# Converting the second half's w_out under attention and keeping it in DRAM

## The chip, the cores and the metric

The kernel runs on one core of a Trainium2 chip. Its engines work from queues of their own: TensorE (PE; its weight loads are listed as PEld), VectorE (DVE), ScalarE (ACT), GpSimd (POOL), and SyncE (SP), which here only issues DMA transfers. Times are device microseconds (us), the median of several runs; a profile is one execution.

## The reference

```python
# attention: 8 batches, 8 heads, 512 local and 32 global tokens, 64 per head
s_ll = where(|i - j| <= 32, q_l k_l^T / 8, -1e9)      # a band of keys
out_l = softmax([q_l k_g^T / 8, s_ll]) [v_g, v_l]     # local tokens
out_g = softmax(q_g [k_g, k_l]^T / 8) [v_g, v_l]      # global tokens
# FFN over 4,352 tokens of 512, d_ff = 2048; weights and products at better than fp32r
h = x @ w_in                                          # 512 x 2048
g = h * erf(softplus(h))
out = g @ w_out                                       # 2048 x 512
```

## The kernel before

**Numbers.** The weights arrive as fp64 and are converted on the chip. A product of the accuracy wanted is made of three fp32r matmuls: each operand is split into a high part (`hi`, rounded) and a low part (`lo`, the rest), and hi x hi, hi x lo and lo x hi are added. `to_fp32` loads a block of 128 x 512 fp64 (`raw`, 524 KB), takes its magnitude on ScalarE and builds the fp32 value on VectorE from the bits (`top`); `split` makes the high part (a copy) and the low part (a subtraction on GpSimd or VectorE).

**Two halves.** The d_ff columns are worked in two halves of 1,024. The first half runs interleaved with attention. `attention` writes its result, transposed, to DRAM (`xsc`, and `xsg` for the global tokens); the tokens are then worked in nine chunks, one for each batch (512 tokens) and a last one of the 256 global tokens. For the first half `unit` multiplies by w_in, `gate` applies the function (two activation tables, each loaded anew), and `project` multiplies by w_out and stores the partial sum (`part`) from a staging tile `os`.

**The second half** takes the chunks in four pairs. Seven products of block sums replace the eight of a pair's first layer: `convert_in` makes the weight blocks and their sums and stores them in DRAM (`wq`), `pair_blocks` loads a pair's tokens (`rx`) and makes the sums and the splits, `products` does the matmuls in banks `pa` to `pd` and folds them on VectorE (`u`, `pair`). `project` multiplies by w_out, loads `part` into an `os` tile, adds, and stores the output. The last chunk (`last_blocks`, `last_unit`; names with `g`) uses four of the seven weight parts.

**Where the w_out of the second half is converted.** `load_unit` writes its parts into the buffers in which the first half's w_out lies, `oh` and `ol` of each of four units, so it can begin only when the first half has projected with that unit. That is at keys 71 to 74, the hand-over between the halves. The tokens of pair 1 wait in addition for three of these units (`AFTER`, `LAST`).

**Order.** Every operation is added with a key, a list of engines that could do it with a cost each, and what it reads and writes. `Program.schedule` plays this through once, before anything runs: at each moment a free engine takes the ready operation with the smallest key, if its buffers are free and its key isn't over 10.4 beyond the first one not done. The order found is written into the program, engine by engine, SP's transfers too. So a cost in these lists moves no work on the chip by itself, but it can change the order of everything. An instruction that waits holds what comes behind it on its engine. A buffer belongs to a tag with a fixed number of copies: `os` has four, `hs` and `sp` seven, `raw` five (raw weights and the tokens `rx` use the same), `wt` and `wr` one.

Of the kernel before, what the change touches and what calls it, by code (L numbers as in the profile page):

```python
# [20 lines left out]
P = 128  # L21
# [10 lines left out]
QLEAD, VLEAD, RLEAD, XLEAD = 0.755, 0.15, 0.011, 2.0  # L32
GOFF, POFF = 1.27, 4.29
WIN, WOUT = (-4.26, -3.26, -2.26, -1.26), (4.0, 5.0, 6.0, 7.0)
CV0, CVS, CVO = (46.5, 54.5), 1.8, (71.0, 72.0, 73.0, 74.0)
QLEAD2, XDEL = 4.0, 1.6
GATE1, GATE2, PROJ1, PROJ2 = (11.0, 17.0), (20.0, 25.0), 15.0, 23.0
LAST = (0, 2, 1)
BIAS, AHEAD = 0.65, 10.4

SLACK, PORT = {"PE": 0.8, "SP": 0.8}, 0.7
# [3 lines left out]
EARLY |= {f"va_0_{h}": ("hs" if h < 4 else "sp", 7) for h in range(8)}  # L45
EARLY |= {f"xT_0_{2 * p + 1}": ("gh", 5) for p in range(4)}
EARLY |= {f"vb_0_{h}": ("xh" if h % 2 == 0 else "xl", 3) for h in range(6)}
QUICK, WLEAD = 0, 0.011
LATER, GFIRST = 12, (-2.0, -1.7)
NORMAL = 1.125 * 2.0**-15  # L50
STRAIGHT = False
# [208 lines left out]
def kernel(  # L260
# [39 lines left out]
    act = lambda *a, **k: pinned(nc.scalar.activation(*a, **k))  # L300
    table = lambda name: pinned(nc.scalar.preload_act_table_set(name))  # L301
    dma = lambda *a, **k: pinned(nc.sync.dma_start(*a, **k))  # L302
    dma_act = lambda *a, **k: pinned(nc.scalar.dma_start(*a, **k))

    class Pin:
        def __init__(self, eng):
# [17 lines left out]
        b.ap = t  # L324
        return b

    def load(key, dst, src, kbytes, deps=(), also=(), quick=False):
        if quick:
            add({"ACT": 0.1}, key, lambda: dma_act(dst.ap, src), reads=deps, writes=[dst, *also], moved=kbytes)
            return  # L330
        add({"SP": 0.06}, key, lambda: dma(dst.ap, src), reads=deps, writes=[dst, *also], moved=kbytes)

    cs = attn.tile([P, 512 + P + 64 + 2], F32, name="cs")
    CS = fixed(cs)
# [21 lines left out]
    def abuf(shape, name, tag, bufs):  # L356
        if name in EARLY:
            tag, bufs = EARLY[name]
            b = Buf(mp, [P, 512 if tag in ("hs", "sp", "gh") else 1024], F32, name, tag, bufs)
            if bufs == 0:  # L360
                b.pool, b.bufs = wpool, 1
            b.view = shape
            return b
        return Buf(attn, shape, F32, name, tag, bufs)

    def psum_a(shape, name):
        return Buf(ps_a, shape, F32, name, "a", 6)

    def attention(b, h, key):
# [103 lines left out]
        if h % 2 == 1:  # L473
            XT = abuf([P, 4, P], f"xT_{nm}", "xT", 1)
            add({"DVE": 0.62},
                key + STEP * 4,
                lambda: dve.transpose(
                    XT.ap.rearrange("p j (t d) -> p j t d", d=WB), XN.ap.rearrange("p t (j d) -> p j t d", d=WB)
                ),
                [XN],  # L480
                [XT],
            )
            rows = xsc[b][P * p : P * p + P, :].rearrange("(j d) (a x) -> a d j x", d=WB, a=4)

            def store():
                for a in range(4):
                    (dma_act if b < QUICK else dma)(rows[a], XT.ap[WB * a : WB * a + WB])

            add({"ACT": 0.4} if b < QUICK else {"SP": 0.24}, key + STEP * 4, store, [XT, ATTN], [XSC[b, p]], moved=262.0)
        if h % 4 == 3:  # L490
            more = b, h // 4, [st["va", i] for i in range(4)], [st["qk", i] for i in range(2)]
            if b == 0 and LATER:
# [9 lines left out]
    def attention_global(b, j, VA, qk, key):  # L502
# [75 lines left out]
        def spread(e):  # L578
# [20 lines left out]
        )  # L599
        XT = abuf([P, 2, SG], f"gxT_{nm}", "gxT", 2)  # L600
        add({"DVE": 0.13, "ACT": 0.22}, key + STEP * 4, lambda e: copy(e, XT.ap.rearrange("p a q -> p (a q)"), X.ap), [X], [XT])
        add({"SP": 0.06},
            key + STEP * 4,
            lambda: dma(
                xsg[256 * j : 256 * j + 256, SG * b : SG * b + SG].rearrange("(a p) q -> p a q", p=P), XT.ap
# [4 lines left out]
        )  # L610

    st, W = {}, {}

    def mbuf(shape, dtype, name, tag, bufs):
        return Buf(mp, shape, dtype, name, tag, bufs)

    def to_fp32(key, src, name, TOP, ABS, deps, lead=RLEAD):

# [46 lines left out]
    def load_unit(kind, src, half, u, hi, lo, key, deps=(), lead=RLEAD):  # L665
# [5 lines left out]
            load_w(key + 0.01 * i, src[half, u, i], f"{kind}_{half}_{u}_{i}", HI, LO, i, deps, lead)  # L671
        W[kind, half, u] = (HI, LO)

    def load_x(ps, c, key):

        n = SL if c < B else B * SG
        X = []
        for i in range(2):
            RAW = mbuf([P, 2 * SL], F32, f"rx_{ps}_{c}_{i}", "raw", RAWS)
            HI = mbuf([P, 2 * SL], F32R, f"xh_{ps}_{c}_{i}", "xh", 3)  # L680
            LO = mbuf([P, 2 * SL], F32R, f"xl_{ps}_{c}_{i}", "xl", 3)
            for t in (RAW, HI, LO):
                t.view = [P, 2, n]
            src = (xsc[c] if c < B else xsg)[2 * P * i : 2 * P * i + 2 * P, :]
            deps = [XSC[c, p] for p in range(2 * i, 2 * i + 2)] if c < B else XSG
            load(key + 0.1 * i, RAW, src.rearrange("(k p) t -> p k t", p=P), 2.048 * n / 2, deps, quick=c < QUICK and ps == 0)
# [98 lines left out]
    def project(ps, c, G, at, order, after=None):  # L785
# [15 lines left out]
        for t in range(nt):  # L801
            for n, rows in enumerate(order):
                need = [x for g, _, v in rows for x in (*G[g], *W["out", ps, v // 2])]
                add(
                    {"PE": 0.685 * len(rows)},
                    at(n) + 0.01 * t,
                    lambda t=t, n=n: mm2(t, n),
                    list(dict.fromkeys(need)) + ([PART[after, t]] if after is not None and n == 0 else []),
                    [OP[t]],
                    heat=1536 * len(rows),  # L810
                )
            k = at(len(order) - 1) + 0.01 * t
            O = mbuf([P, DM], F32, f"os_{ps}_{c}_{t}", "os", 4)
            if ps == 0:
                add({"ACT": 0.58, "DVE": 0.69}, k, lambda e, t=t, O=O: copy(e, O.ap, OP[t].ap), [OP[t]], [O])
                add({"SP": 0.06},
                    k,
                    lambda t=t, O=O: dma(part[c][P * t : P * t + P, :], O.ap),
                    [O],
                    [PART[c, t]],  # L820
                    moved=262.0,
                )
            else:
                load(k - NU + 2, O, part[c][P * t : P * t + P, :], 262, [PART[c, t]])
                add({"DVE": 0.69},
                    k,
                    lambda t=t, O=O: dve.tensor_tensor(O.ap, OP[t].ap, O.ap, ALU.add),
                    [OP[t]],
                    [O, PART[c, t]],
                )  # L830
                add({"SP": 0.06}, k, lambda t=t, O=O: dma(out_rows(c, t), O.ap), [O], [fixed(None)], moved=262.0)

    class Late:

# [9 lines left out]
    for u in range(NU):  # L844
        load_unit("in", w_in, 0, u, (wpool, f"ih{u}"), (wpool, f"il{u}"), WIN[u], (), WLEAD)
        load_unit("out", w_out, 0, u, (wpool, f"oh{u}"), (wpool, f"ol{u}"), WOUT[u])

    def head_key(n):
        for (n0, k0), (n1, k1) in zip(HKEYS, HKEYS[1:]):
# [14 lines left out]
    def convert_in(u, key):  # L864
# [48 lines left out]
        for r, HL in enumerate(quads):  # L913
            for x, t in enumerate(HL):
                add(
                    {"SP": 0.06},
                    k + 0.6,
                    lambda x=x, t=t, q=2 * u + r: dma(wq[q][x], t.ap.bitcast(F32)),
                    [t],
                    [WQ[2 * u + r, x]],  # L920
                    moved=918.0,
                )
        return {2 * u + r: HL for r, HL in enumerate(quads)}


    def quad_weights(name, q, key):
        HL = [Buf(wb_pool, [P, 7, 2, P], F32R, f"wq{x}_{name}", f"q{x}", 2) for x in range(2)]
        for x, t in enumerate(HL):
            add(
                {"SP": 0.06},  # L930
                key,
                lambda x=x, t=t: dma(t.ap.bitcast(F32), wq[q][x]),
                [WQ[q, x]],
                [t],
                moved=918.0,
            )
        return HL

# [142 lines left out]
    def last_unit(q, X, key):  # L1081


        QH, QL = quad_weights(f"g{q}", q, key - QLEAD2)
        n = B * SG
        HP = Buf(ps_h, [P, 2, n], F32, f"h_g{q}", "h", 2)

# [33 lines left out]
    for u in range(2):  # L1121
        first = convert_in(1 - u, CV0[u])
    for n, u in enumerate((0, 2, 1, 3)):
        load_unit("out", w_out, 1, u, (wpool, f"oh{u}"), (wpool, f"ol{u}"), CVO[n], [ATTN])


    s0 = 17 * NU
    turns, ACTS = (), fixed(None)
    AFTER = {0: first[0], 1: [W["out", 1, u][1] for u in LAST]}
    for pr in range(B // 2):  # L1130
        s = s0 + 4 * NU * pr
        X = pair_blocks(pr, s - XDEL)
# [5 lines left out]
        order = [[(v, 0, v) for v in (2 * u, 2 * u + 1)] for u in (0, 2, 1, 3)]  # L1138
        for us, c, g, at in ((one, 2 * pr, GATE1, PROJ1), (two, 2 * pr + 1, GATE2, PROJ2)):
            G = {}  # L1140
            for h in range(2):
                turn = fixed(None)
                G |= gate(1, c, us[4 * h : 4 * h + 4], s + g[h], turns, [turn], [ACTS])
                turns = [turn]
            project(1, c, G, lambda n: s + at + 2 * n, order, c - 1 if c else None)
    s = s0 + 4 * NU * (B // 2)
# [83 lines left out]
```

## Time and profile before

| | |
|---|---|
| median of 3 runs (lowest, highest) | 957.44 us (957.0, 959.39) |
| the profiled execution: its time, its span | 959.59 us, 957.6 us |
| mean granted clock of TensorE | 0.982 |
| busy: TensorE, VectorE, ScalarE, GpSimd | 919.5, 650.2, 528.2, 401.7 us |
| moved by DMA | 168 MB, mean 175 GB/s |

The span is the time from the first to the last instruction; the run's time contains what lies around it. Matmuls overlap, so that the mean duration of one (about 390 ns for 512 columns) is longer than the distance between two. Names of tiles stand without their numbers: `top_out` is the fp32 value made of a w_out block, `wouth` and `woutl` its parts, `op` the bank of a projection, `o` that of attention's value product, `va` and `vb` its value tiles.

### The profile page before, as it was taken

To read this page: it belongs to the slowest core of one execution; us is meant where nothing else is said; L and a number is where in the kernel's file an instruction comes from. 1 tells how busy PE (TensorE), PEld (TensorE's weight loads), DVE (VectorE), ACT (ScalarE), POOL (GpSimd) and SP (SyncE) were. 2 spreads that over 40 slices of the span, in tenths; PEclk is the share of its full clock that TensorE was granted. 3 is DMA by queue.
4 is the path that set the end of the run, shared out by engine and by line. 5 is a ranking of instruction groups with operands and counts; after the bars stand their busy time and mean duration, and the time that the engine had idled before them with its cause. 6 is when DMAs were issued, how large, how long until landed. Compare 5 with 4: busy or idle time off the path is not lost.

```text
span 957.6 us, 22226 instructions
## 1 busy us (share of the span) xinstructions
PE 919.5 (96%) x8938; PEld 740.7 (77%) x8938; DVE 650.2 (68%) x1496; ACT 528.2 (55%) x868; POOL 401.7 (42%) x293
## 2 busy tenths in 40 slices
PE   8988899999989999999999999989999999999996
PEld 6666677777777777778888887767888888888885
DVE  4998889747856675855767799789656446544462
ACT  2547757455735545645765772657528445742850
POOL 1334645323313253312555683266537537521240
PEclk9999899999989999999999999989999999999999
DMA  9886577445864653724242453751742734334622
GB/s 345 290 292 206 185 228 239 135 118 180 253 196 122 214 183 94 237 53 146 88 186 78 173 201 120 284 189 43 287 165 78 252 135 183 121 144 165 231 89 88
DMA packets 86078, 168.00 MB, mean 175 GB/s; under 512 B 12888, under 2 KB 38488, under 8 KB 85976
## 3 DMA queue, kind: packets, MB, share of 16 engines
q1 hardware_dynamic: 85976, 166.60, 51.2%
q8 instruction: 70, 1.15, 0.5%
q14 instruction: 32, 0.26, 0.1%
HBM read 132.48 MB, written 34.08 MB: 174 GB/s over the span
## 4 chain that ended last, share of the span: by engine, by line
PE 71%; DVE 14%; DMA 9%; SPq 2%; issue 2%; ACT 1%; POOL 1%; DVEq 0%; ACTq 0%
PE op L298 33%; PE h L298 15%; PE pc L298 4%; PE pd L298 4%; PE pa L298 3%; PE o L298 3%; DVE top_out L311 2%; PE t L299 2%; PE s L298 2%; SPq L302 2%; PE pb L298 2%; DMA vb<-in_vB_dram 2%; DMA k<-in_kE_dram 2%; DVE xl_T L311 2%; DVE sp L311 1%
## 5 line engine op out<-in xcount | busy, mean ns | idle before, releaser
L298 PE MATMUL op<-wouth,gh 128*128 128x512 f32 x544 | 217.9, 401 | 0.0
L298 PE MATMUL op<-wouth,gl 128*128 128x512 f32 x544 | 212.8, 391 | 0.1
L298 PE MATMUL op<-woutl,gh 128*128 128x512 f32 x544 | 212.6, 391 | 0.0
L311 POOL TENSOR_TENSOR gl<-sp,gh 128x512 fp32r<-128x512 f32 x69 | 98.9, 1437 | 139.1 <-ACT gh L300 75.7
L300 ACT ACTIVATE gh<-sp 128x512 fp32r<-128x512 f32 x103 | 63.2, 628 | 106.9 <-PE op L298 75.9
L298 PEld LDWEIGHTS op<-wouth,gh 128*128 128x128 f32 x544 | 102.6, 189 | 23.2 <-issue 1.8
L298 PEld LDWEIGHTS op<-wouth,gl 128*128 128x128 f32 x544 | 102.4, 188 | 22.4 <-DVE gl L311 0.5
L311 POOL TENSOR_TENSOR sm<-sm,mx 128x512 f32<-128x512 f32 x41 | 45.4, 1113 | 174.6 <-DVE mx L311 125.0
L298 PEld LDWEIGHTS op<-woutl,gh 128*128 128x128 f32 x544 | 102.7, 189 | 19.5
L301 ACT ACT_TABLE_LOAD x90 | 115.5, 1283 | 2.3 <-PEq L1217 0.7
L298 PE MATMUL h<-xh,winh 128*128 128x512 f32 (+1 forms) x288 | 114.5, 398 | 0.0
L298 PE MATMUL h<-xl,winh 128*128 128x512 f32 (+1 forms) x288 | 111.0, 385 | 0.0
L298 PE MATMUL h<-xh,winl 128*128 128x512 f32 (+1 forms) x288 | 111.0, 385 | 0.0
L311 DVE TENSOR_TENSOR gl<-sp,gh 128x512 fp32r<-128x512 f32 x67 | 64.6, 969 | 37.3 <-ACT gh L300 33.7
L311 POOL TENSOR_TENSOR sp<-sp,hs 128x512 f32<-128x512 f32 x41 | 61.2, 1512 | 38.7 <-ACT sp L300 38.7
L300 ACT ACTIVATE sp<-sp 128x512 f32<-128x512 f32 x136 | 74.9, 620 | 0.4
L311 DVE CUSTOM_DVE_ANT_0 sm<-s,cs 128x128 f32<-128x128 f32 x256 | 57.1, 284 | 24.7 <-PE s L298 18.3
L300 ACT ACTIVATE hs<-h 128x512 f32<-128x512 f32 x49 | 29.3, 597 | 67.6 <-PE h L298 67.6
L298 PEld LDWEIGHTS h<-xh,winh 128*128 128x128 f32 x288 | 55.7, 193 | 11.3 <-issue 1.0
L298 PEld LDWEIGHTS h<-xh,winl 128*128 128x128 f32 x288 | 55.5, 193 | 11.4 <-issue 0.4
L298 PEld LDWEIGHTS h<-xl,winh 128*128 128x128 f32 x288 | 55.6, 193 | 9.6
L300 ACT ACTIVATE sm<-sm 128x512 f32<-128x512 f32 x64 | 39.3, 630 | 41.0 <-POOL sm L311 35.0
(181 smaller groups left out, 1844.9 us busy)
## 6 DMA issues: line engine op xcount, KB each, us to landing
wq<-wq SPq DMA_DIRECT2D x28, 896.0 KB, 6.3
vb<-in_vB_dram SPq DMA_DIRECT2D x64, 325.0 KB, 4.1
rx<-xsc SPq DMA_DIRECT2D x32, 512.0 KB, 7.6
va<-in_vA_dram SPq DMA_DIRECT2D x64, 195.0 KB, 3.6
k<-in_kE_dram SPq DMA_DIRECT2D x32, 384.0 KB, 5.8
q<-in_qT_dram SPq DMA_DIRECT2D x32, 272.0 KB, 4.7
part<-os SPq DMA_DIRECT2D x34, 256.0 KB, 3.0
os<-part SPq DMA_DIRECT2D x34, 256.0 KB, 3.7
```

The costliest lines, as they stand in the source:

```text
L298: pe = lambda n, *a, **k: pinned(nc.tensor.matmul(n, *a, **k))
L299: tr = lambda *a, **k: pinned(nc.tensor.transpose(*a, **k))
L300: act = lambda *a, **k: pinned(nc.scalar.activation(*a, **k))
L301: table = lambda name: pinned(nc.scalar.preload_act_table_set(name))
L302: dma = lambda *a, **k: pinned(nc.sync.dma_start(*a, **k))
L311: return lambda *a, **k: pinned(f(*a, **k))
```

## The change

The second half's w_out is converted by `keep_unit` at keys 20 to 37.5, in the middle of attention, into two `os` tiles a block, and stored in DRAM (`wo`, 16 stores of 262 KB). At keys 71 to 74 `fetch_unit` loads the finished parts (8 transfers of 524 KB) into the same `oh` and `ol` buffers as before. Pair 1's tokens no longer wait for it. Chunk 0 of the second half has three gates instead of two (2, 2 and 4 tiles, the first ones earlier). The last chunk's staging tiles carry the tag `hs`. Its weight loads take four of seven parts. And the planner counts 0.35 us of SP for each DMA, where it counted 0.06.

```diff
-LAST = (0, 2, 1)
+KEEP, KSTEP, FIRST = 20.0, 2.5, (6.0, 9.0)
+SPT = 0.35
...
-        add({"SP": 0.06}, key, lambda: dma(dst.ap, src), reads=deps, writes=[dst, *also], moved=kbytes)
+        add({"SP": SPT}, key, lambda: dma(dst.ap, src), reads=deps, writes=[dst, *also], moved=kbytes)
...
-            add({"ACT": 0.4} if b < QUICK else {"SP": 0.24}, key + STEP * 4, store, [XT, ATTN], [XSC[b, p]], moved=262.0)
+            add({"SP": 4 * SPT}, key + STEP * 4, store, [XT, ATTN], [XSC[b, p]], moved=262.0)
...
+    wo = [[dram.tile([P, 2, 512], F32, name=f"wo{u}_{x}") for x in range(2)] for u in range(NU)]
+    WO = {}
+
+    def keep_unit(u, key):
+
+        for i in range(2):
+            nm, k = f"k_out_{u}_{i}", key + KSTEP * i
+            TOP = View(mbuf([P, 512], F32, f"top_{nm}", ("wt", "wr")[i % 2], 1))
+            H, L = (View(mbuf([P, 512], F32R, f"{x}_{nm}", "os", 4)) for x in ("hi", "lo"))
+            to_fp32(k, w_out[1, u, i], nm, TOP, H, (), 1.0)
+            split(k, TOP, H, L)
+            for x, t in enumerate((H, L)):
+                WO[u, i, x] = fixed(None)
+                add(
+                    {"SP": SPT},
+                    k + 0.2,
+                    lambda x=x, t=t, i=i: dma(wo[u][x][:, i, :], t.ap().bitcast(F32)),
+                    [t.buf],
+                    [WO[u, i, x]],
+                    moved=262.0,
+                )
+
+    def fetch_unit(u, key):
+        parts = [Buf(wpool, [P, 2, 512], F32R, f"wout{x}_1_{u}", f"o{x}{u}") for x in "hl"]
+        for x, t in enumerate(parts):
+            add(
+                {"SP": SPT},
+                key,
+                lambda x=x, t=t: dma(t.ap.bitcast(F32), wo[u][x]),
+                [WO[u, i, x] for i in range(2)],
+                [t],
+                moved=524.0,
+            )
+        W["out", 1, u] = parts
...
-            O = mbuf([P, DM], F32, f"os_{ps}_{c}_{t}", "os", 4)
+            O = mbuf([P, DM], F32, f"os_{ps}_{c}_{t}", *(("os", 4) if ps == 0 or c < B else ("hs", 7)))
...
+    for u in range(NU):
+        keep_unit(u, KEEP + 2 * KSTEP * u)
...
-    def quad_weights(name, q, key):
+    def quad_weights(name, q, key, n=7):
...
-                lambda x=x, t=t: dma(t.ap.bitcast(F32), wq[q][x]),
+                lambda x=x, t=t: dma(t.ap[:, :n].bitcast(F32), wq[q][x][:, :n]),
...
-                moved=918.0,
+                moved=131.0 * n,
...
-        QH, QL = quad_weights(f"g{q}", q, key - QLEAD2)
+        QH, QL = quad_weights(f"g{q}", q, key - QLEAD2, S1 + 1)
...
-        load_unit("out", w_out, 1, u, (wpool, f"oh{u}"), (wpool, f"ol{u}"), CVO[n], [ATTN])
+        fetch_unit(u, CVO[n])
...
-    AFTER = {0: first[0], 1: [W["out", 1, u][1] for u in LAST]}
+    AFTER = {0: first[0]}
...
-            for h in range(2):
+            for a, z, at_z in ((0, 2, FIRST[0]), (2, 4, FIRST[1]), (4, 8, g[1])) if c == 0 else ((0, 4, g[0]), (4, 8, g[1])):
                 turn = fixed(None)
-                G |= gate(1, c, us[4 * h : 4 * h + 4], s + g[h], turns, [turn], [ACTS])
+                G |= gate(1, c, us[a:z], s + at_z, turns, [turn], [ACTS])
```

The other changed lines write `SPT` for 0.06 at the remaining DMAs and drop a second DMA queue that was switched off (`QUICK = 0`).

## Rows read from the trace of the kernel before

**Rows 1.** The page's head.
```profile
span 957.6 us, 22226 instructions
```

**Rows 2.** Stretch; busy (instructions) PE, PEld, DVE, ACT, POOL; clock, DMA share, GB/s.
```profile
264.00:432.00 168.00, 164.05 (x2300) 127.44 (x2300) 106.96 (x363) 86.17 (x148) 48.50 (x37) 0.98 0.50 156
...
570.00:672.00 102.00, 93.65 (x387) 74.96 (x386) 88.90 (x110) 56.67 (x91) 49.44 (x33) 0.95 0.42 161
672.00:888.00 216.00, 216.00 (x960) 179.07 (x959) 114.20 (x151) 105.62 (x163) 102.77 (x70) 1.00 0.46 167
...
276.00:288.00 12.00, 9.13 (x103) 7.41 (x92) 5.61 (x25) 5.10 (x11) 2.08 (x2) 0.72 0.62 201
```

**Rows 3.** TensorE's waits, 570 to 672 us, then after 880: total, times, longest.
```profile
PE pc L298 <- DVE pair L311: 4.3, 2, 3.9
PE pa L298 <- DVE u L311: 3.0, 1, 3.0
PE pd L298 <- DVE pair L311: 0.8, 1, 0.8
...
PE h_g L298 <- DMA wq_g<-wq: 1.8, 1, 1.8
```

**Rows 4.** VectorE's timeline: start, us, operation, out<-in; in brackets the idle time before.
```profile
613.38 1.56 DVE L311 TENSOR_SCALAR top_out<-raw_out 128x512 int32<-128x512 int32 x1
...
624.03 0.69 DVE L311 TENSOR_TENSOR pair<-u,pc 128x512 f32<-128x512 f32 x1
...
954.00 0.69 DVE L311 TENSOR_TENSOR os<-op,os 128x512 f32<-128x512 f32 x1 [5.01 <-DMA os<-part]
```

**Rows 5.** TensorE's timeline: a late value product, two hand-over gaps, the end.
```profile
279.45 0.41 PE L298 MATMUL o<-va,pt 128*32 128x65 f32 x3 [2.87 <-issue]
...
624.77 0.79 PE L298 MATMUL pc<-xh_B,wq 128*128 128x512 f32 x1 [3.87 <-DVE pair L311]
...
630.05 0.49 PE L298 MATMUL op<-wouth,gh 128*128 128x512 f32 x1
...
646.97 0.51 PE L298 MATMUL pa<-xh_B,wq 128*128 128x512 f32 x1 [3.00 <-DVE u L311]
...
650.95 0.40 PE L298 MATMUL pb<-xl_T,wq 128*128 128x512 f32 x1
...
949.23 0.39 PE L298 MATMUL op<-wouth,gl 128*128 128x512 f32 x1
```

**Rows 6.** Tile top_out, 560 to 672 us: busy by engine; durations min/median/max in ns.
```profile
560.00:672.00 112.00, 27.84 (x38) 3.74 (x6) 5.84 (x4) 0.95 0.43 161
...
L311 DVE SCALAR_TENSOR_TENSOR top_out<-raw_out,top_out x16: 691/693/1756, 582.2 to 628.6; 128x512 int32<-128x512 int32 x16
L311 DVE TENSOR_SCALAR top_out<-raw_out x8: 414/421/1565, 581.3 to 627.4; 128x512 int32<-128x512 int32 x8
```

**Rows 7.** SP's timeline of DMA issues: start, us, out<-in, count.
```profile
247.11 0.42 SPq L302 DMA_DIRECT2D k<-in_kE_dram  x1
...
273.76 1.98 SPq L302 DMA_DIRECT2D xsc<-xT  x4
276.15 0.83 SPq L302 DMA_DIRECT2D va<-in_vA_dram  x2
...
614.80 0.38 SPq L302 DMA_DIRECT2D raw_out<-in_w_out_dram  x1
615.27 4.41 SPq L302 DMA_DIRECT2D rx<-xsc  x4
```

**Rows 8.** The page's DMA issues: count, KB each, us to landing.
```profile
wq<-wq SPq DMA_DIRECT2D x28, 896.0 KB, 6.3
...
part<-os SPq DMA_DIRECT2D x34, 256.0 KB, 3.0
```

**Rows 9.** The chain that ended last: start, us, what.
```profile
891.41 8.67 DMA wq_g<-wq
...
944.93 6.02 DMA out_dram<-os
```

More of the change, by code (lines that the diff above doesn't have):

```diff
@@ L47 @@
 EARLY |= {f"vb_0_{h}": ("xh" if h % 2 == 0 else "xl", 3) for h in range(6)}
-QUICK, WLEAD = 0, 0.011
+WLEAD = 0.011
 LATER, GFIRST = 12, (-2.0, -1.7)
@@ L302 @@
     dma = lambda *a, **k: pinned(nc.sync.dma_start(*a, **k))
-    dma_act = lambda *a, **k: pinned(nc.scalar.dma_start(*a, **k))
     class Pin:
@@ L325, in fixed, with load @@
         return b
[L327 to L330, printed above, removed]
-        add({"SP": 0.06}, key, lambda: dma(dst.ap, src), reads=deps, writes=[dst, *also], moved=kbytes)
+    def load(key, dst, src, kbytes, deps=(), also=()):
+        add({"SP": SPT}, key, lambda: dma(dst.ap, src), reads=deps, writes=[dst, *also], moved=kbytes)
     cs = attn.tile([P, 512 + P + 64 + 2], F32, name="cs")
@@ L364, in abuf, with mbuf @@
         return Buf(attn, shape, F32, name, tag, bufs)
+    def mbuf(shape, dtype, name, tag, bufs):
+        return Buf(mp, shape, dtype, name, tag, bufs)
     def psum_a(shape, name):
@@ L486, in store @@
                 for a in range(4):
-                    (dma_act if b < QUICK else dma)(rows[a], XT.ap[WB * a : WB * a + WB])
-            add({"ACT": 0.4} if b < QUICK else {"SP": 0.24}, key + STEP * 4, store, [XT, ATTN], [XSC[b, p]], moved=262.0)
+                    dma(rows[a], XT.ap[WB * a : WB * a + WB])
+            add({"SP": 4 * SPT}, key + STEP * 4, store, [XT, ATTN], [XSC[b, p]], moved=262.0)
         if h % 4 == 3:
@@ L601, in attention_global @@
         add({"DVE": 0.13, "ACT": 0.22}, key + STEP * 4, lambda e: copy(e, XT.ap.rearrange("p a q -> p (a q)"), X.ap), [X], [XT])
-        add({"SP": 0.06},
+        add({"SP": SPT},
             key + STEP * 4,
@@ L612 @@
     st, W = {}, {}
-    def mbuf(shape, dtype, name, tag, bufs):
-        return Buf(mp, shape, dtype, name, tag, bufs)
     def to_fp32(key, src, name, TOP, ABS, deps, lead=RLEAD):
@@ L685, in load_x @@
             deps = [XSC[c, p] for p in range(2 * i, 2 * i + 2)] if c < B else XSG
-            load(key + 0.1 * i, RAW, src.rearrange("(k p) t -> p k t", p=P), 2.048 * n / 2, deps, quick=c < QUICK and ps == 0)
+            load(key + 0.1 * i, RAW, src.rearrange("(k p) t -> p k t", p=P), 2.048 * n / 2, deps)
             k = key + 0.1 * i + STEP * 2
@@ L812, in project @@
             k = at(len(order) - 1) + 0.01 * t
-            O = mbuf([P, DM], F32, f"os_{ps}_{c}_{t}", "os", 4)
+            O = mbuf([P, DM], F32, f"os_{ps}_{c}_{t}", *(("os", 4) if ps == 0 or c < B else ("hs", 7)))
             if ps == 0:
                 add({"ACT": 0.58, "DVE": 0.69}, k, lambda e, t=t, O=O: copy(e, O.ap, OP[t].ap), [OP[t]], [O])
-                add({"SP": 0.06},
+                add({"SP": SPT},
                     k,
@@ L830, in project @@
                 )
-                add({"SP": 0.06}, k, lambda t=t, O=O: dma(out_rows(c, t), O.ap), [O], [fixed(None)], moved=262.0)
+                add({"SP": SPT}, k, lambda t=t, O=O: dma(out_rows(c, t), O.ap), [O], [fixed(None)], moved=262.0)
     class Late:
@@ L915, in convert_in @@
                 add(
-                    {"SP": 0.06},
+                    {"SP": SPT},
                     k + 0.6,
@@ L929, in quad_weights @@
             add(
-                {"SP": 0.06},
+                {"SP": SPT},
                 key,
-                lambda x=x, t=t: dma(t.ap.bitcast(F32), wq[q][x]),
+                lambda x=x, t=t: dma(t.ap[:, :n].bitcast(F32), wq[q][x][:, :n]),
                 [WQ[q, x]],
                 [t],
-                moved=918.0,
+                moved=131.0 * n,
             )
```

## The prediction

> **What bounds the kernel now.** I read the page first, then a table of stages, then the waits of TensorE, then the engines' timelines around each wait.
>
> The span is 957.6 us [rows 1]. The profiled run took 959.59 us, about 2 us above the median of 957.44; the launch adds the same to both kernels, so I take every saving off the median. In the stage table [rows 2] the reader sees that TensorE never stops from 672 to 888 us: 960 matmuls in 216.00 us, 0.225 us each. That is what a stage costs when nothing is in its way, and nothing in this change takes a matmul away. So only gaps can be won. From 570 to 672 us, where the first half hands over to the second, TensorE is busy 93.65 of 102 us: 8.35 us idle. From 264 to 432 us, under attention, it is busy 164.05 of 168.
>
> The waits of the hand-over name one releaser, VectorE [rows 3]: 4.3 (3.87 and a second of 0.43), 3.0 and 0.8 us. VectorE's timeline shows why the longest lasted 3.87 us: from 613.38 us it works on `top_out`, the conversion of w_out, and the fold into `pair` for which TensorE needs its PSUM bank starts only at 624.03 [rows 4]. A gap costs twice. After it, the 12 matmuls from 624.77 to 630.05 us start 0.44 us apart instead of 0.225: the 1.2 GHz level, not the 2.4 GHz one [rows 5], so 5.28 - 2.70 = 2.6 us more. After the 3.00 us wait it is 10 matmuls from 646.97 to 650.95: 3.98 - 2.25 = 1.7 us. The hand-over thus loses 8.35 + 4.3 = 12.65 us. (387 matmuls at 0.225 us would fill 87.1 of the 102 us, which says 14.9; some records may be missing, so I use the smaller number.)
>
> **The change part by part.**
>
> *w_out leaves the hand-over.* The instructions on `top_out` take 27.84 us of VectorE from 560 to 672 us, with 3.74 of ScalarE and 5.84 of GpSimd [rows 6]; there VectorE is busy 88.90 of 102 us [rows 2]. All of it goes. The first wait (0.83, `pd`) and the 3.87 us wait sit behind it directly. The 3.00 us wait does so through a queue: pair 1's four `rx` loads were issued at 615.27, behind the last `raw_out` load at 614.80 [rows 7], because they had to wait for the conversion of three units and for staging buffers of the same tag. Their blocks were then built on VectorE in one run while TensorE waited for `u`. After the change the loads depend on neither. They can go out once pair 0's staging is free, and at the later hand-overs between pairs, where no conversion stands in the way, TensorE loses nothing from 672 to 888 us [rows 2].
>
> In its place come 8 fetches of 524 KB, the byte count of the 8 raw loads they replace. The page has 6.3 us for a landing of 896 KB and 3.0 for 256 KB [rows 8], so a fetch lands in 3 to 6 us. What follows is no conversion but the projection itself. The extra gate of chunk 0 adds two table loads, about 2.6 us of ScalarE, which is busy 56.67 of 102 us there [rows 2]: hidden, and at most 2.6 us if the last gate before chunk 0's second half of rows is on the path. What is late next? With VectorE down to some 61 of 102 us, pair 1's block building, which can't start before pair 0's last products release the tiles. I leave 2 us of gap for it (bounds 0 and 5.1, the last being the 3.00 us wait, its 1.7 of slow clock and that wait of 0.4). Gain 12.65 - 2.0 = 10.6.
>
> *Under attention.* Keys 20 to 37.5 are those of heads 41 to 59 of 64. The `k` of heads 42 and 43 is issued at 247.11 us [rows 7], so this lies between some 245 and 400 us, mostly in the stage of 264 to 432. Each of 8 blocks brings an Abs on ScalarE, one TENSOR_SCALAR and three SCALAR_TENSOR_TENSOR on VectorE, a copy and a subtraction. At the medians [rows 6] that is 0.42 + 3 x 0.69 = 2.5 us of VectorE a block, 20 us in all; with the subtractions and copies that fell to it before it was 28. VectorE has 168 - 106.96 = 61.0 us idle in that stage, ScalarE 81.8 and GpSimd 119.5 [rows 2]: hidden, unless it holds up something in order. The transfers are 8 loads of 524 KB and 16 stores of 262 KB, 8.4 MB beside the 156 GB/s x 168 us = 26.2 MB there; the DMA share would go from 0.50 to about 0.66. On SP's queue 24 issues at 0.41 us (two `va` in 0.83, [rows 7]) are 10 us of 168.
>
> The order matters more than the sums. Each store waits on SP for a ScalarE, VectorE or GpSimd result; behind it stand `va`, `vb`, `k` and `q`, for which TensorE waits. What that costs is in the trace: at 273.76 us four `xsc` stores stood ahead of two `va` loads, these were issued at 276.15, and the value matmuls started at 279.45, after 2.87 us of nothing, 3.3 us behind the issue [rows 5, 7]; the row names no releaser, so that it was this load is my reading. The 12 `h` matmuls behind it ran at the lower level (clock 0.72 from 276 to 288, [rows 2]), about 12 x 0.2 = 2.4 us: 5.3 us for one such stall. The stores also take two of the four `os` buffers, so an eviction can wait a landing, 3.0 us [rows 8]. Bounds 0 and 10.6 (two stalls); I take 2, nearer the low end, since TensorE waited for a load like that once in these 168 us.
>
> The trace shows how VectorE slows down when GpSimd works beside it: the same TENSOR_SCALAR takes 0.41 to 1.57 us, SCALAR_TENSOR_TENSOR 0.69 to 1.76 [rows 6]. If every conversion instruction met that, a block would cost 1.57 + 3 x 1.76 + 1.76 (a subtraction as slow) = 8.6 us, 69 us in all, more than the 61.0 idle. The page "SBUF — State Buffer" of the Trainium skill (section "Who interferes with whom") states this as a rule: VectorE with two SBUF inputs contends with a GpSimd instruction that reads SBUF, and whoever issues first blocks the other fully. It speaks against moving this work beside attention; by it the conversion would cost up to the 69 us, with the time of the rival below, and not the 28. The total of 27.84 us, measured with GpSimd at 49 of 102 us, against 48.5 of 168 under attention [rows 2], keeps me at 28.
>
> *The planner's 0.35 us for a DMA on SP.* No instruction changes, but the order does. The trace has about 0.41 us an issue; the planner counted 0.06, so ten queued transfers came over 3 us later than it planned. The stall just described is such a lateness. It may go (5.3 us) or not (0): I take half, 2.6.
>
> *The end.* The last matmul starts at 949.23 and ends near 949.6 [rows 5]. The last addition starts at 954.00, after 5.0 us of waiting for `os<-part` [rows 4]: with four `os` buffers for six tiles, the load had to wait for an output store issued at 944.93 that took 6.02 us [rows 9]. With the tags of `hs`, of which there are seven and by then few in use, the load can be early; the addition then starts at about 949.65. Gain 954.00 - 949.65 = 4.35.
>
> *The last weights.* 4 of 7 parts: each of 8 loads falls from 918 to 524 KB. Before, TensorE waited 1.8 us [rows 3] for a transfer that took 8.67 us on the chain [rows 9]; at 4/7 it is 3.7 us shorter. I take the whole 1.8 as gone (bounds 0, if the order and not the size is what is late, and 1.8).
>
> Sum: 10.6 + 4.35 + 1.8 + 2.6 - 2.0 = 17.35; 957.44 - 17.35 = **940 us** (against the profiled run's own 959.59 it is 942). At the bounds, with everything well: 12.65 + 4.35 + 1.8 + 5.3 = 24.1, 933. With everything ill but two stalls: 7.5 + 4.35 - 10.6 = 1.2, 956.
>
> **The rivals.**
> - *The hand-over closes only in part.* Against it: it is the conversion that stands in VectorE's timeline. For it: pair 1's blocks were built in one run of 14 us with TensorE waiting, and building them is not shortened. Gain 7.5 + 4.35 + 1.8 - 2 + 0: 946.
> - *The new stores hold SP under attention; slower.* Place 245 to 400 us, 5.3 us a stall. It decides from the fourth one, beyond the 19 us won elsewhere; with all of that won and five stalls it is 957.4 - 19 + 26.5 = 965. For it: one such stall exists already and 24 waiting DMAs are added. Against it: the planner now counts their time.
> - *VectorE fills up under attention.* If the conversion costs 69 us there, VectorE is full for 168 us, and TensorE loses as in the hand-over, 12.65 us in 102, so 20.8: 957.44 - 10.6 - 4.35 - 1.8 + 20.8, about 961. Against it: the smaller GpSimd share. The skill page's lock, named above, is what would do it.
> - *Fetches stand behind `wq` loads* that wait for products, so chunk 0 has no w_out until they move. Then the 12.65 us mostly stay, the rest is won: 951.
> - *The true SP cost mends more of attention* than this one stall: up to 6 us more, 934.
>
> **How the numbers follow.** 940 has 0.52, part-closed 0.20, stores on SP 0.07, VectorE full 0.04, late fetches 0.05, more mended 0.09, nothing to measure 0.03. About 0.3%, 2.9 us, is what a measurement can tell from no change. Faster: 0.52 + 0.20 + 0.05 + 0.09 = 0.86; same 0.03; slower 0.11. The range that leaves some 2 in 10 out goes from 933, the good bound, to 952, past the late fetches.
>
> **What would show it.** In the new profile: no `top_out` work of half 1 between 570 and 672 us; pair 1's `rx` issued some 20 us before pair 0's last products; no VectorE wait over 1 us at the hand-over and the clock at 1.00 throughout; `os<-part` no longer in the last 8 us; no wait for `wq_g`. It would be wrong if 245 to 400 us shows new waits of `o` or `s` for loads, each with a stretch of low clock, or if TensorE waits for the fetched `wout` tiles.

## The result, and the profile after

The changed kernel takes 945.65 us (median of 4 runs, 944.67 to 946.68); the kernel before took 958.41 us beside it on the same chip (4 runs, 957.0 to 960.14). The ratio is 0.9866, 95% interval 0.9844 to 0.9888: 12.8 us less, where I had forecast 17.4. The profiled execution took 945.86 us, at a mean granted clock of 0.991 (0.982 before).

The head of the page of the changed kernel answers to [rows 1]. Its matmul helper is now line 299, its VectorE helper still 311, its DMA helper 303.

```profile
span 944.1 us, 22303 instructions
```

The stage table of the changed kernel, columns as in [rows 2]: attention, the stall near 279 us, the hand-over, the stage between pairs, and a long stretch over both.

```profile
264.00:432.00 168.00, 166.02 (x2294) 128.31 (x2287) 120.87 (x380) 98.52 (x175) 54.88 (x42) 1.00 0.60 187
276.00:288.00 12.00, 11.81 (x194) 9.45 (x192) 10.19 (x33) 6.84 (x16) 4.33 (x3) 1.00 0.63 192
560.00:664.00 104.00, 102.01 (x448) 83.33 (x447) 70.78 (x75) 58.10 (x90) 54.07 (x34) 1.00 0.49 182
664.00:872.00 208.00, 208.00 (x920) 172.22 (x919) 114.22 (x154) 110.85 (x169) 103.36 (x72) 1.00 0.46 165
600.00:936.00 336.00, 336.00 (x1529) 280.08 (x1528) 184.00 (x240) 181.37 (x272) 152.45 (x103) 1.00 0.45 161
```

The hand-over is closed: TensorE idles 2.0 of 104 us where it idled 8.35 of 102, the clock stays at 1.00, and from 600 to 936 us there is no gap at all. VectorE is busy 70.78 us in place of 88.90, where some 61 had been forecast. The waits of TensorE from 560 to 700 us answer to [rows 3]:

```profile
PE pa L299 <- DVE c L311: 1.1, 1, 1.1
PE pd L299 <- DVE xl_T L311: 0.7, 1, 0.7
PE pc L299 <- DVE pair L311: 0.2, 1, 0.2
```

SP's timeline answers to [rows 7]: pair 1's `rx` go out at 592 and 597 us, not at 615, among the fetches of the kept w_out; the last line is the end, six output stores and nothing before them that waits.

```profile
592.46 0.37 SPq L303 DMA_DIRECT2D rx<-xsc  x1
595.87 0.32 SPq L303 DMA_DIRECT2D wouth<-wo  x1
...
596.77 1.41 SPq L303 DMA_DIRECT2D rx<-xsc  x3
...
606.75 0.32 SPq L303 DMA_DIRECT2D wouth<-wo  x1
...
927.84 12.57 SPq L303 DMA_DIRECT2D out_dram<-os  x6
```

TensorE's last matmul and VectorE's additions answer to the last lines of [rows 5] and [rows 4]. The additions follow TensorE (releaser `PE op`), no longer a load of `os<-part`; no wait for `wq_g` is left either.

```profile
938.93 0.39 PE L299 MATMUL op<-wouth,gl 128*128 128x512 f32 x1
```

```profile
938.00 0.69 DVE L311 TENSOR_TENSOR os<-op,os 128x512 f32<-128x512 f32 x1 [0.67 <-PE op L299]
939.36 0.69 DVE L311 TENSOR_TENSOR os<-op,os 128x512 f32<-128x512 f32 x1 [0.67 <-PE op L299]
```

The conversion now stands under attention, from 201 to 352 us. Its tile, with durations in ns as in [rows 6]; over the whole span the instructions on it take 28.20 us of VectorE.

```profile
0.00:960.00 960.00, 28.20 (x35) 3.16 (x5) 11.18 (x8) 0.99 0.54 180
...
L311 DVE SCALAR_TENSOR_TENSOR top_k_out<-raw_k_out,top_k_out x16: 691/693/1666, 201.4 to 342.8; 128x512 int32<-128x512 int32 x16
L311 DVE TENSOR_SCALAR top_k_out<-raw_k_out x8: 403/424/1343, 200.9 to 339.7; 128x512 int32<-128x512 int32 x8
L311 DVE SCALAR_TENSOR_TENSOR top_k_out<-hi_k_out,top_k_out x8: 674/694/1772, 202.9 to 350.7; 128x512 f32<-128x512 f32 x8
```

**Where the 13.5 us between the two spans went.** I cut both spans at two marks that TensorE's timeline gives. The last `h` matmul of the first half starts at 559.1 us before and 562.6 after: 3.5 us lost. From there to the start of the last matmul it is 390.13 us before and 376.37 after: 13.8 won. From the start of the last matmul to the end of the span it is 8.37 and 5.17: 3.2 won.

### The profile page after: what moved, and what is told of

It reads as the page before. It is cut to its first block, busy times and chain, and to the rows that moved or that the text cites. A ratio compares the mean times of both kernels' runs of the same rounds, so it can differ in the third digit from the quotient of the medians.

```text
span 944.1 us, 22303 instructions
## 1 busy us (share of the span) xinstructions
PE 914.6 (97%) x8937; PEld 736.0 (78%) x8937; DVE 643.0 (68%) x1484; ACT 536.0 (57%) x895; POOL 401.8 (43%) x295
## 3 DMA queue, kind: packets, MB, share of 16 engines
q8 instruction: 70, 1.15, 0.5%
## 4 chain that ended last, share of the span: by engine, by line
PE 79%; DVE 9%; issue 2%; DMA 1%; SPq 0%; ACT 0%; DVEq 0%
PE op L299 37%; PE h L299 16%; PE pc L299 4%; PE pd L299 4%; PE pa L299 4%; DVE top_out L311 3%; PE o L299 2%; PE s L299 2%; PE pb L299 2%; PE t L300 2%; PE h_g L299 1%; PE go L299 1%; PE ga L299 1%; DVE sm L311 1%; PE gt L300 1%
## 5 line engine op out<-in xcount | busy, mean ns | idle before, releaser
L311 POOL TENSOR_TENSOR gl<-sp,gh 128x512 fp32r<-128x512 f32 x66 | 92.7, 1409 | 111.7 <-ACT gh L301 70.0
L311 POOL TENSOR_TENSOR sm<-sm,mx 128x512 f32<-128x512 f32 x43 | 49.0, 1149 | 131.9 <-DVE mx L311 77.3
L311 DVE TENSOR_TENSOR gl<-sp,gh 128x512 fp32r<-128x512 f32 x70 | 70.7, 1019 | 38.6 <-ACT gh L301 37.3
L311 POOL TENSOR_TENSOR sp<-sp,hs 128x512 f32<-128x512 f32 x46 | 68.3, 1505 | 55.0 <-ACT sp L301 55.0
L301 ACT ACTIVATE hs<-h 128x512 f32<-128x512 f32 x44 | 26.2, 595 | 62.0 <-PE h L299 62.0
```

What stands on the lines that cost most here:

```text
L311: return lambda *a, **k: pinned(f(*a, **k))
```

## The experiments

Each ratio is to the kernel before, timed beside it on the same chip. Four parts of the change can be made alone, so I began with these.

**The SP cost alone.** The kernel before with one number changed wherever a DMA is planned:

```diff
-        add({"SP": 0.06}, key, lambda: dma(dst.ap, src), reads=deps, writes=[dst, *also], moved=kbytes)
+        add({"SP": 0.35}, key, lambda: dma(dst.ap, src), reads=deps, writes=[dst, *also], moved=kbytes)
```

> The kernel before with one edit: the planner counts 0.35 us of SP for each DMA and not 0.06. Theory 1 (the new order under attention is what costs the 3.5 us by which the changed kernel's first half ends later): 961 to 964 us, with TensorE losing more before 190 us than in the kernel before. Theory 2 (the moved conversion costs them; the true SP cost mends the late value load at 279 us): 953 to 957 us, and no stall near 279 us.

Measured: 968.87 us, ratio 1.0087 (1.0062 to 1.0111): 8.6 us slower; neither theory had that. The stall near 279 us was gone (TensorE busy 12.00 of the 12 us from 276), but the hand-over grew (96.73 of the 115 us from 565 to 680, before 106.65). SP's timeline of this kernel shows pair 1's four `rx` now ahead of the last `raw_out`, and TensorE's waits from 560 to 700 us show what it cost:

```profile
619.29 2.46 SPq L303 DMA_DIRECT2D rx<-xsc  x4
621.87 0.45 SPq L303 DMA_DIRECT2D raw_out<-in_w_out_dram  x1
```

```profile
PE pc L299 <- DVE c L312: 14.2, 2, 12.2
PE pc L299 <- DVE pair L312: 2.2, 3, 1.2
```

The last block of the conversion then ran at 637 to 649 us, amid pair 1's block building. A truer cost in the plan is not a gain by itself.

**Everything but the SP cost.** The changed kernel with `SPT = 0.06`.

> The changed kernel with the planner's SP cost back at 0.06 us. Theory 1: 941 to 943 us, the first half's last matmul at 558 to 560 us. Theory 2: 946 to 949 us, that matmul at 562 us or later.

Measured: 954.17 us, ratio 0.9935 (0.9914 to 0.9956), slower than both theories had it. With the conversion moved, the same cost that lost 8.6 us alone is worth some 6.6, by the difference to the changed kernel's ratio (0.0069 of 960 us; with the two intervals some 3 us either way).

**The conversion alone.** The kernel before with `keep_unit`, `fetch_unit` and the shorter `AFTER`; SP cost, gates and the end as before.

> The kernel before with the conversion moved under attention and the fetches, and nothing else of the change (SP cost 0.06, two gates for chunk 0, four staging buffers, seven weight parts). Both theories have the hand-over of 12.65 us closed to within 2. Theory 1: 946 to 948 us. Theory 2: 949 to 951 us. If the third gate of chunk 0 is what fills TensorE at the hand-over, TensorE still waits there for over 3 us: 950 or more, with the waits between 600 and 660 us.

Measured: 959.61 us, ratio 0.9986 (0.9969 to 1.0003): no change that can be measured, where the theories had 946 to 951. The hand-over closed here too (TensorE busy 112.35 of 115 us from 565 to 680, 106.65 before), but the last first-half `h` came at 569.2, 10 us later than before. All of the gain was given back under attention, and this kernel's VectorE timeline shows the place:

```profile
273.26 0.68 DVE L311 TENSOR_TENSOR gl<-sp,gh 128x512 fp32r<-128x512 f32 x1
303.06 0.29 DVE L311 CUSTOM_DVE_ANT_0 sm<-s,cs 128x128 f32<-128x128 f32 x1 [29.12 <-PE t L300]
```

VectorE had nothing for 29 us, because TensorE was given 34 us of `h` and `op` matmuls in one piece, from 268.2 us on. The longest such piece between 190 and 436 us is 8.3 us in the kernel before and 6.9 in the changed one (worked out from the starts in TensorE's timeline). SP's front DMA waited for a product behind that piece; SP's waits in this kernel, 190 to 360 us:

```profile
SPq L303 <- PE o L299: 42.6, 13, 29.1
```

TensorE itself was full meanwhile. The loss came afterwards, in attention. Two stretches, of this kernel and then of the changed one:

```profile
270.00:300.00 30.00, 30.00 (x134) 24.86 (x133) 3.94 (x4) 12.16 (x19) 7.62 (x6) 1.00 0.08 30
300.00:348.00 48.00, 38.64 (x753) 30.45 (x753) 37.93 (x132) 31.21 (x58) 21.13 (x17) 0.89 0.78 257
```

```profile
270.00:300.00 30.00, 28.88 (x420) 22.83 (x419) 24.59 (x71) 18.19 (x35) 14.16 (x10) 1.00 0.74 244
300.00:348.00 48.00, 47.75 (x688) 37.35 (x687) 36.84 (x113) 32.17 (x56) 15.55 (x12) 1.00 0.72 222
```

From 300 to 348 us 9.4 us are idle at a clock of 0.89, against 0.25 at 1.00.

**The two ends alone.** The kernel before with the last chunk's staging in the tags of `hs` and 4 of 7 parts of the last weights.

> The kernel before with the last chunk's staging under the tag of hs and four of seven weight parts for it, and nothing else. By the prediction 4.35 + 1.8 = 6.15 us less: 952.3 us. By what the new profile shows of the tail (3.2 us less from the last matmul to the end) and the whole 1.8: 953.4. If the order and not the size made the last weights late, the wait stays: 955.

Measured: 953.84 us, ratio 0.993 (0.991 to 0.9949): 6.4 us, against 4.35 + 1.8 = 6.15 forecast.

**Without the conversion's work.** The changed kernel, with the first half's w_out stored in place of a converted second half; it leaves out the 8 loads and all the work of the conversion, and has 8 stores of 524 KB:

```diff
-            to_fp32(k, w_out[1, u, i], nm, TOP, H, (), 1.0)
-            split(k, TOP, H, L)
...
+        for x, t in enumerate(W["out", 0, u]):
...
+                lambda x=x, t=t: dma(wo[u][x], t.ap.bitcast(F32)),
```

> The changed kernel without the conversion of the second half's w_out: neither its 8 loads nor any instruction on top_out and its parts; the first half's converted w_out is stored instead, in 8 stores of 524 KB at the same planned times (so the second half multiplies with the wrong weights: this asks only for time). Open question: of the 4.2 us that the sum missed (12.8 us won, 17.35 forecast), are they paid for the conversion under attention? Theory 1 (yes, the moved conversion costs some 4 us there, twice what I put down): the kernel comes out near 941 to 942, ratio to before 0.982. Theory 2 (attention differs only by how the plan falls out, and by some us from one execution to the next; the conversion is hidden): 945 to 947, ratio 0.986 to 0.988, with the last first-half h matmul still near 562 us.

Measured: 943.43 us, ratio 0.984 (0.9816 to 0.9864), 2.2 us below the changed kernel (2.5 by the ratios); the intervals overlap. The conversion costs 0 to some 5 us under attention, the middle of it where I had put it (2.0). It is hardly what the forecast missed, though the upper end isn't excluded; and this kernel, too, has an order of its own, which can be a part of the difference.

**Two gates for chunk 0.** The changed kernel with `for a, z, at_z in ((0, 4, g[0]), (4, 8, g[1]))` for every chunk.

> The changed kernel with two gates for chunk 0 of the second half, of four units each, as before, in place of three (two, two and four units). Theory 1 (the third gate hides: its two table loads on ScalarE cost nothing and chunk 0's projection was not waiting for the first gate): ratio 0.986 to 0.988, no change that can be told from the changed kernel, TensorE's hand-over from 565 to 680 us still with less than 3 us of waits. Theory 2 (with w_out already there, chunk 0's projection now starts as early as its gate allows, and the early gate of two units is what lets it): 3 to 6 us slower, ratio 0.990 to 0.993, and a TensorE wait of that size for g of chunk 0 between 590 and 625 us.

Measured: 947.95 us, ratio 0.9868 (0.9844 to 0.9892), as the changed kernel. The third gate neither costs nor brings anything that can be measured here, which means less than some 3 us.

**The rx loads freed, the conversion left where it was.** The kernel before with one dependency less:

```diff
-    AFTER = {0: first[0], 1: [W["out", 1, u][1] for u in LAST]}
+    AFTER = {0: first[0]}
```

> The kernel before, with one dependency taken off: pair 1's four rx loads no longer wait for the conversion of three units of w_out; the conversion itself stays at the hand-over. My prediction laid the 3.00 us wait for u (with its 1.7 us of slow clock and the small wait of 0.4) on these loads being late. Theory 1 (that is so): the rx loads go out some 15 to 20 us before 615 us, the wait of pa for u is gone, the 3.87 us wait stays, and the kernel gains up to 5 us, ratio 0.995 to 0.997. Theory 2 (VectorE is what is full there, so that the blocks, built earlier, only push the conversion later): ratio 0.999 to 1.003, and the waits grow somewhere else in the hand-over.

Measured: 965.94 us, ratio 1.0078 (1.005 to 1.0106): 7.5 us slower; neither theory had that. One of the four loads went out 8 us earlier, the other three did not. In SP's timeline the last raw block now falls behind them (before it went out at 614.80): as I read it, they take its staging tiles. TensorE's waits from 560 to 700 us (the three largest) move to what is built late:

```profile
607.37 0.39 SPq L302 DMA_DIRECT2D rx<-xsc  x1
...
615.51 2.03 SPq L302 DMA_DIRECT2D rx<-xsc  x3
620.04 0.35 SPq L302 DMA_DIRECT2D raw_out<-in_w_out_dram  x1
```

```profile
PE pd L298 <- DVE xl_T L311: 5.1, 2, 4.5
PE op L298 <- POOL gl L311: 2.5, 1, 2.5
PE op L298 <- ACT gh L300: 1.9, 1, 1.9
```

It is the same picture as with the SP cost alone: at the hand-over the five staging tiles and VectorE are shared by conversion and block building, and putting the one first makes the other late. Of these kernels, only those without the conversion there have neither late.

**The conversion and the SP cost, without the ends and the third gate.** The conversion alone, with 0.35.

> The kernel before, with the conversion moved and the planner's 0.35 us for an SP transfer, but without the two changes at the end and without the third gate. So far the cost alone made it 8.6 us slower, and the conversion alone changed nothing that could be measured. Theory 1 (the two need each other: only with room in the plan for SP's issues does the conversion fit under attention without holding up loads, and the gain of the hand-over shows): the changed kernel's 12.8 us less the 6.4 us that the ends gave alone, so 6 us faster than before, ratio 0.993 to 0.995, hand-over waits under 3 us, last first-half h near 562 us. Theory 2 (they add up: 8.6 slower and 0.6 faster): ratio 1.005 to 1.010.

Measured: 951.49 us, ratio 0.9917 (0.9892 to 0.9943). Alone the two are 8.6 us slower and nothing; together they are 8.6 us faster (6 us by the theory that they need each other). Beside the 6.4 us of the ends that makes 15, within what the intervals allow for the 12.8.

**Three plans more.** The changed kernel with the old SP cost for keys under 8 (`ways = {"SP": ways["SP"] * 0.06 / SPT}` in the planner); with the conversion later (`KEEP, KSTEP = 42.0, 1.5`); with `SPT = 0.41`.

> The changed kernel, with the planner's 0.35 us for an SP transfer only for work with keys from 8 on (some 165 us and later); before that the old 0.06. In the traces so far TensorE was busy 38.6 to 39.6 of the 40 us from 100 to 140 us in the kernel before and in the one with rx freed, and 36.8 to 37.2 in the changed kernel and the two of its variants read there, all with 0.35, though the moved conversion begins only later. Theory 1 (the higher cost makes a worse order in the early part, 2 to 3 us, and a better one where the stores are): 942 to 944, ratio 0.982 to 0.984, with 39 of 40 us busy from 100 to 140 us. Theory 2 (every change to the plan gives another order, and the early part's 2 us are one draw of many): no better than the changed kernel, ratio 0.985 or more.

> The changed kernel with the conversion of w_out planned from key 42 on, in steps of 1.5, in place of 20 in steps of 2.5: after attention, under the first half's last chunks, some 355 to 440 us, where VectorE is busy 52 of 85 us and TensorE waits for nothing. Theory 1 (under attention the conversion costs the 2.2 us by which the kernel without it is ahead, and in the new place nothing): 943 to 944, ratio about 0.984. Theory 2 (the new place runs into the conversion of w_in that follows, and the hand-over opens again): 948 or more, ratio 0.989 or more, with hand-over waits over 4 us.

> The changed kernel with 0.41 us as the planner's cost of an SP transfer, which is what the trace shows for an issue, in place of 0.35. Theory 1 (a truer cost gives a better order): 943 to 946, ratio 0.984 to 0.987. Theory 2 (the cost decides only which of many orders falls out): several us away from the changed kernel on either side, ratio under 0.983 or over 0.990.

The first took 943.37 us, ratio 0.9824 (0.9799 to 0.9849), the best of all that compute the whole reference; its interval just touches that of the changed kernel. TensorE is busy 39.83 of the 40 us from 100 to 140 us there, 36.93 in the changed kernel, as the first theory wanted. The third took 944.3, ratio 0.984 (0.9812 to 0.9868), not to be told from the changed kernel. The second took 952.75, ratio 0.994 (0.9913 to 0.9966): moved to a place that looked free, the conversion cost 7 us more. Its hand-over had 4.8 us of waits (2.0 in the changed kernel), as the second theory had it. TensorE again has a piece of `h` and `op` of 30.1 us, from 406.0 us on. Between 355 and 565 us it has these waits, where the changed kernel has 0.6 us; the two short ones come within 25 us of the piece's end, the long one 73 us behind it:

```profile
PE h L299 <- DVE hs L311: 3.2, 1, 3.2
PE go L299 <- DVE gt L311: 1.5, 1, 1.5
PE gx L299 <- DVE xg L311: 1.3, 1, 1.3
```

By the marks, in a run of 950.64 us, its last first-half `h` comes 1.7 us later than in the changed kernel, and from there to the last matmul it takes 2.9 us more.

**The stores on ScalarE's queue.** Everything but the SP cost, as above, in the very same order, with one line changed:

```diff
-                    lambda x=x, t=t, i=i: dma(wo[u][x][:, i, :], t.ap().bitcast(F32)),
+                    lambda x=x, t=t, i=i: pinned(nc.scalar.dma_start(wo[u][x][:, i, :], t.ap().bitcast(F32))),
```

> The changed kernel with the old SP cost of 0.06 in the planner (ratio 0.9935 so far, SP held for 29.1 us by one load under attention), in the very same order on every engine; only the 16 stores of the converted parts are issued from ScalarE's queue in place of SP's, at the same place of the order. It asks what holds attention up there. Theory 1 (the stores on SP: loads stand behind stores that wait for the conversion, as my rival had it): the loads go out earlier, TensorE is busy 45 or more of the 48 us from 300 to 348 us in place of some 38, and the kernel comes near the changed one, ratio 0.987 to 0.989. Theory 2 (the planner's order: TensorE is given a block of h and op of over 30 us, VectorE has nothing meanwhile, and SP's front load waits for a product behind that block; the stores are not what holds it): ratio 0.992 to 0.996, SP still held for 25 us or more by a product o, and TensorE still some 38 of 48 us busy behind it.

Measured: 956.4 us, ratio 0.9967 (0.9945 to 0.999), no better than with the stores on SP (0.9935). SP still waits for a product, now 36.2 us at most, and TensorE's two stretches are as before. SP's longest waits and then the stretches, of this kernel:

```profile
SPq L303 <- PE o L299: 57.1, 12, 36.2
```

```profile
270.00:300.00 30.00, 30.00 (x134) 24.83 (x133) 4.82 (x4) 11.61 (x18) 7.61 (x7) 1.00 0.11 36
300.00:348.00 48.00, 36.94 (x745) 29.09 (x744) 37.38 (x131) 31.45 (x57) 20.75 (x16) 0.89 0.77 247
```

So the stores are not what holds attention up in these kernels. What is left is the order: each of the four kernels with a piece of over 30 us of `h` and `op` (the conversion alone, everything but the SP cost, the conversion later, this one) is 6 us or more behind the changed kernel by its ratio; the kernel before, the changed one, the one without the conversion's work, and those with 0.35 alone, 0.41 or the late 0.35 have no piece over 8.3 us. No run breaks such a piece up in an otherwise equal order, so that the piece is the cause is read from the waits and from this pairing, and not tested.

## Why the prediction was right, and where it was not

The time alone decides little: 945.65 us lies nearest to the rival of a hand-over that closes only in part (946). The profile has to say which terms came true. That the sum came so near is in part luck: it was added term by term, and the runs show that its largest term, the hand-over, comes out in the time only together with the planner's cost, on which 2.6 us were put.

**The hand-over: right.** 12.65 us were counted as lost there and 2 us left over; 2.0 us of waits are left, the longest of 1.1 us just over the 1 us that was named as a sign. With the last weights I had 10.6 + 1.8 = 12.4 us; the marks give 13.8. That the conversion was the cause is shown by the kernel with the conversion alone, which closes the hand-over. With its work on VectorE its raw blocks leave the staging tiles, too; these two the runs don't part (the dependency of `rx`, taken off alone, won nothing).

**The 3.00 us wait: half right.** I had two reasons why `rx` was late, the dependency on three converted units and the staging tiles of the same tag. With the dependency taken off, three of the four loads were no earlier. So what frees them should be that the raw blocks leave the staging tiles; no run changes these alone.

**The conversion's price: right.** 28 us of VectorE were forecast, 28.20 measured; 2 us on TensorE's path forecast, 2.2 (0 to some 5) by the kernel without the work. The place was not: 245 to 400 us was forecast, 201 to 352 measured. The longest instructions took 1.67 and 1.77 us against medians of 0.69. Of the 32 that write `top_k_out`, 8 took over 0.8 us, and all 8 ran while GpSimd was in a TENSOR_TENSOR; of the other 24, 22 met none. Two pairs of VectorE in the changed kernel, the first with GpSimd idle, the second beside the GpSimd row that follows:

```profile
300.92 1.42 DVE L311 SCALAR_TENSOR_TENSOR top_k_out<-raw_k_out,top_k_out 128x512 int32<-128x512 int32 x2
...
341.07 3.36 DVE L311 SCALAR_TENSOR_TENSOR top_k_out<-raw_k_out,top_k_out 128x512 int32<-128x512 int32 x2
```

```profile
339.46 4.42 POOL L311 TENSOR_TENSOR sp<-sp,hs 128x512 f32<-128x512 f32 x3
```

By the Trainium skill's page "SBUF — State Buffer" (section "Who interferes with whom") VectorE with two SBUF inputs contends with a GpSimd instruction that reads SBUF. The trace agrees, but GpSimd was busy only 61.61 of the 165 us from 190 to 355, and most instructions kept their usual time. The rival built on 69 us is out.

**The ends: right in sum.** 6.15 us forecast, 6.4 measured alone (4.9 to 8.6 by the interval). The profile accounts for 5.0 of it, the wait of 1.8 and the tail; that the sum is so near is luck in part. In the profile the tail is 3.2 us shorter, not 4.35: the addition does follow TensorE at once, but from its end to the end of the span it takes 944.1 - 940.05 = 4.05 us, where it took 957.6 - 954.69 = 2.91. The last two additions, and so the last two stores, now come 1.36 us apart and not 5.7; whether that is why, I did not test.

**The planner's SP cost: this step failed.** I had written "It may go (5.3 us) or not (0): I take half, 2.6", a price for one stall. The stall did go: from 276 to 288 us TensorE is busy 11.81 in place of 9.13, at 1.00 in place of 0.72. But its price was no fixed one. The kernels with the ends alone and with rx freed have the order of the kernel before up to here and the same gap (3.14 and 3.19 us, before 2.87), yet the clock of these 12 us, the third number from the end, is 1.00 and 0.86, so the 2.4 us of slow clock in the 5.3 don't come every time:

```profile
276.00:288.00 12.00, 9.26 (x134) 7.41 (x134) 7.08 (x27) 8.47 (x16) 2.68 (x3) 1.00 0.74 215
```

```profile
276.00:288.00 12.00, 8.81 (x199) 7.17 (x198) 6.59 (x30) 4.33 (x11) 2.08 (x2) 0.86 0.74 235
```

Above all, a cost in the planner is a new order for the whole program, and what it is worth depends on everything else in the plan: 8.6 us slower alone, some 6.6 us faster with the conversion moved. In the two profiles attention as a whole came out 3.5 us longer by the marks, where 2.0 - 2.6 = -0.6 was forecast, and this is nearly all that is missing there of the 17.35 (4.1 here, 1.15 in the tail, and 1.4 more than forecast in the hand-over). TensorE's busy time in two stretches, first of the kernel before, then of the changed one, of the one without the conversion's work, and of the one with the late SP cost:

```profile
0.00:190.00 190.00, 174.89 (x3109) 135.06 (x3110) 159.50 (x535) 107.04 (x199) 81.37 (x65) 0.96 0.73 240
190.00:355.00 165.00, 160.84 (x2486) 125.99 (x2488) 109.05 (x387) 88.61 (x147) 52.62 (x40) 0.98 0.58 181
```

```profile
0.00:190.00 190.00, 171.51 (x3084) 130.82 (x3085) 162.34 (x534) 109.73 (x204) 77.61 (x63) 0.96 0.73 238
190.00:355.00 165.00, 161.41 (x2441) 126.36 (x2445) 129.56 (x399) 96.38 (x174) 61.61 (x47) 0.99 0.73 230
```

```profile
0.00:190.00 190.00, 172.67 (x3093) 131.89 (x3094) 164.70 (x537) 111.06 (x206) 78.83 (x65) 0.96 0.74 242
190.00:355.00 165.00, 162.50 (x2494) 125.51 (x2493) 111.25 (x389) 82.27 (x142) 51.82 (x39) 1.00 0.64 204
```

```profile
0.00:190.00 190.00, 173.57 (x3105) 133.74 (x3106) 157.85 (x533) 106.03 (x198) 80.74 (x65) 0.96 0.72 236
190.00:355.00 165.00, 159.83 (x2358) 124.42 (x2358) 132.45 (x397) 95.88 (x164) 65.09 (x46) 0.99 0.70 227
```

The reader sees that the conversion's own stretch is not where the changed kernel is behind; it is the first 190 us, before the conversion starts, where the new order loses 3.4 us. How much of that is the order can't be settled from one profile each: the kernel with two gates has the changed kernel's order on TensorE up to the hand-over, and 174.40 us there. With the old cost kept for the early part the kernel is 2.3 us faster by the medians and 4 by the ratios, at the edge of what can be told, as that reading wants, but it has a stall after 264 us again (busy 86.95 of 91 us to 355, changed kernel 89.62), so the early part alone doesn't explain it.

**The rival on SP's queue: real, but elsewhere and by another cause.** With the old SP cost SP is held 29 us under attention, and that costs as much as the hand-over gave. I had the stores as the cause; the run with them on ScalarE's queue says no. What the waits point to is the planner's order, in which TensorE gets over 30 us of projection while attention stands still. Why the planner makes that piece with some costs and not with others stays open. The fetches behind `wq` and a full VectorE did not come.

## What to carry to other kernels

- Where one engine's work stands in front of another engine's at a stage change, moving it to an earlier stage can win nearly all of the gap, and here, where the earlier stage had twice the room, the price was small; but read the order that results, not only the idle shares: the same work in a place that looked free cost 7 us more.
- Two edits that go through a planner don't add up. Time each alone and both together before a gain is put down to one of them; here one was +8.6 us alone and some -6.6 us in company.
- When a queue is seen waiting, ask what the thing at its front waits for, and whether the engine behind that was given something else first. Moving the other traffic off the queue changed nothing here.

## What the runs showed that I had not expected

- The same order takes different times under attention. The last first-half `h` starts at 559.1 and 555.2 us in two kernels with one order up to there (the one before, and the ends alone), and at 562.6, 559.3 and 564.9 us in three others (the changed one, two gates, conversion and SP cost). The means are 557.2 and 562.2 us, so that the changed order is behind here is likely, but by how much is open. From 680 to 890 us nothing like it is seen: TensorE is busy 210.00 of 210 us in every one of them. So one profile can't tell a 3 us effect under attention.
- A TensorE that is full for 30 us can be the start of a loss: it was busy 30.00 of 30 us while VectorE had 3.94, and gave back 9.4 us in the next 48.
